# A 7x7 circular convolution on one core: scratch loads one group per round in the last tile, a weight group's preparation half a round earlier

## The chip, the core and the metric

The kernel runs on one core of a Trainium2 chip. The core has five engines with their own instruction streams: TensorE (PE), VectorE (DVE), ScalarE (ACT), GpSimd (POOL) and SyncE (SP), which here issues nearly all DMAs. Engines meet at semaphores. The time is the device time of one execution in microseconds (us), and lower is better. Before the change the median of eight runs is 281.08 us (280.29 to 283.76).

## The reference

```
H = W = 224;  C = 96;  K = 7          # x: (1, H, W, C) bf16, w: (K, K, C, C) bf16
wp = pad(w, H and W up to 224)
Yf = einsum('bhwi,hwio->bhwo', rfft2(x), rfft2(wp))
y  = irfft2(Yf)                       # bf16
```

So y is the circular convolution of a 224x224 image of 96 channels with a 7x7 kernel, 96 channels in and out, summed over the input channels.

## The kernel before

**The algorithm.** Rows (h) are cut in eight blocks of 28, each seen through a window of 34 rows. Along h the kernel uses a real Fourier transform of length 34, done as matmuls; it gives 17 frequencies s (`NS`), each with a real and an imaginary part, the first with two real ones. Along w it convolves directly, with the columns split in even and odd ones, which saves a quarter of the taps. A complex product is done with three real ones, so the transformed weights of a frequency take three slots: two parts, and their difference.

**The stages.** The width is cut in seven tiles t of 32 columns (`NT` = 7, `TL` = 6 is the last).

- *Weights*: `prep_jobs(gi)` (line 333) transforms the weights of a group of frequencies, 12 jobs of eight matmuls for groups 2 to 5, each copied from a PSUM bank to `WF`. `w_sub(gi, half)` (line 369) makes the difference slots on DVE, one half of the output channels each. `PGRP` lists six groups; group 5, the fifth after the first one, has frequencies 14 to 16.
- *A*, `a_jobs(t)`: transform of x along h, matmuls with the constant `Fm`, into `xf`.
- *J planes*, `jit(t, g)`: sums and differences of xf for three frequencies, three DVE instructions a group.
- *B*, `b_round(t, s, ...)` (line 485): all products of one frequency, 33 matmuls of 96 columns in two PSUM banks. ACT scales three of the sums (tile `tt_`), DVE makes `u` and `v`, and POOL (sometimes DVE) adds them to `yf`. After each third round `put_y` stores yf to scratch in DRAM (`scr`, in the last tile `scra` for rounds 0 to 8 and three `scrb` for the rest).
- *C*, `c_jobs(t)`: `load_t` reads the scratch back, turned round so that frequencies lie on partitions (tile `tt`), in six groups of two to four DMAs. `c_bank` does the inverse transform, a matmul with `Gm` (G in the code), copies the result to `yo`, and `put_o` stores it to the output.
- *The end*: C of the last tile is done differently. Rounds 0 to 8 are loaded from scra into `tl_a` (the xf buffer that is then free; line 828), rounds 9 to 16 from scrb by `load_b` into `tl_b`. Each of 16 output pieces is the sum of two matmuls, `first` with `GA` (built in Fm once A is over) and `second` with `GB`. Between the first eight `first` and the first `second` stand `WARM` filler matmuls (line 857), which add zeros.

**The order of work.** All engines run in program order, and the program is written round by round. Tiles 0 and 1 run interleaved, tile 1 four rounds (`LAG`) behind; a round r of the loop is then b_round of tile 0 and b_round of tile 1. The later tiles run alone. `add(a, b, jobs)` spreads a list of jobs over the half rounds a to b, and `pace` runs what is due, in the middle (`mid`) or at the end (`end`) of a b_round. `planes` are DVE jobs put between v and the POOL sum; the sum waits for them.

**The queue of scratch loads.** `queue_c(t)` puts the six groups of tile t into `pend`, at round 3 of the next tile, and `pump` (line 676) issues those for which one of the six tt buffers (`NTT`) is free. It runs again after every finished group of C. `late[0]` is 0 throughout. All DMAs, those on ACT's queue too, keep the program's order (`dorder`), and SP executes them one after another: one that waits holds those behind it. In the last tile rounds 9 to 14 are stored from ACT's queue (`puts`), the rest from SP's.

**What the change touches.** `WARM` (line 42), `pump` and `queue_c` (676 to 683), the call of pump in c_jobs (663), the half rounds of group 5's preparation and the round of its second difference (743, 744), and in the tile loop the Fm clear and its four DMAs (`g_parts`, line 617, called at 823), queue_c (821) and the loads of tl_a (828 to 833).

Of the kernel before, what the change touches and what calls it, by code (L numbers as in the profile page):

```python
# [16 lines left out]
NS = L // 2  # L17
# [21 lines left out]
CQ = {2: (10, 2), 3: (8, 4), 4: (6, 7), 5: (3, 9), 6: (1, 5)}  # L39
NXN = 2  # L40
NP2 = 0
WARM = 16


def slot(s, part):
    return part if s == 0 else 2 + 3 * (s - 1) + part
# [3 lines left out]
def kernel(  # L50
# [10 lines left out]
    TL = NT - 1  # L61
# [37 lines left out]
    def bank():  # L99
        return pools["psb"].tile([128, 512], F32, name="pb")  # L100
# [6 lines left out]
    def apart(key, zone, r, keep=None):  # L107
        for z, q in parts.setdefault(key, []):
            if z != zone and not (keep and z in keep) and q.engine != r.ins.engine:
                tc.declare_no_dep(r.ins, q, reason="disjoint parts of one tile")  # L110
        parts[key].append((zone, r.ins))
        return r

    def evac(out_ap, in_ap, n):
        if tail[0]:
            return tail_evac(out_ap, in_ap, n)
        cv, ca = 180 + 1.0 * n, 160 + 0.85 * n
        if clamp[0]:
            top = max(load.values()) - 2000
            for k in load:  # L120
                load[k] = max(load[k], top)
        if load["v"] + cv <= load["a"] + ca:
            load["v"] += cv
            return VE.tensor_copy(out=out_ap, in_=in_ap)
        load["a"] += ca
        return SE.copy(out=out_ap, in_=in_ap)
# [27 lines left out]
    SA = SL[1]  # L154
# [178 lines left out]
    def prep_jobs(gi):  # L333
        s0, s1 = PGRP[gi]
        ns = s1 - s0
        full = gi == 0
        if full:
            ncol = NSLOT_OF(s0, s1) * NTAP
        else:
            ncol = 2 * ns * NTAP  # L340
        nb = C // NB
        hb = NB // 2
        assert NB * ncol <= 512 and C2 % hb == 0

        def mk_(ob):
            def f():
                pw = bank()
                pv_ = pw[:, 0:NB * ncol].rearrange("p (k h q) -> p k h q", h=2, q=ncol)
                if full:
                    ev = Em[:, :, slot(s0, 0):slot(s0, 0) + ncol // NTAP, :].rearrange("p h a t -> p h (a t)")  # L350
                else:
                    ev = Em[:, :, slot(s0, 0):slot(s1 - 1, 2) + 1, :].rearrange("p h (s r) t -> p h s (r t)", r=3)[:, :, :, 0:2 * NTAP]
                for k in range(hb):
                    o = ob * hb + k
                    TE.matmul(pv_[:, k], lhsT=wqx[0:PW2, o:o + 127 * C + 1:C], rhs=ev, start=True, stop=True)
                pv_ = pv_[0:C]
                o0, o1 = ob * hb, (ob + 1) * hb
                if full:
                    wv = WF[0:C, slot(s0, 0):slot(s0, 0) + ncol // NTAP].rearrange("i a t (h o) -> i (a t) h o", h=2)
                    r = evac(wv[..., o0:o1], pv_.rearrange("i k h q -> i q h k"), NB * ncol)  # L360
                    apart(("W", gi), ob, r)
                    return r
                wv = WF[0:C, slot(s0, 0):slot(s1 - 1, 2) + 1].rearrange("i (s r) t (h o) -> i s (r t) h o", r=3, h=2)
                apart(("W", gi), ob, evac(wv[:, :, 0:2 * NTAP, :, o0:o1],
                      pv_.rearrange("i k h (s q) -> i s q h k", s=ns), NB * ncol))
            return f
        return [mk_(ob) for ob in range(nb)]
# [16 lines left out]
    def NSLOT_OF(s0, s1):  # L384
        return slot(s1 - 1, 2) + 1 - slot(s0, 0)
# [253 lines left out]
    def c_jobs(t):  # L639
        jobs = []  # L640
        for h in range(2):
            for gi in range(3):
                j0, nj = CG[gi]
                hold = {}

                def mk_(ks, done, h=h, gi=gi, j0=j0, nj=nj, hold=hold):
                    def f():
                        if ks[0] == 0:
                            hold["yo"] = yo_pool.tile([4 * B, PXC * C], BF16, name="yo")
                        tt = tt_tiles[(t, gi, h)]  # L650
                        yo = hold["yo"]
                        for k in ks:
                            c_bank(tt, yo, k, 3 if gi < 2 or h == 0 or k == 0 else 2)
                        if not done:
                            return
                        if gi < 2:
                            put_o(t, yo, 0, j0, nj, 8 * h, 8 * h + 8, 0)
                        else:
                            put_o(t, yo, 0, j0, nj, 6 * h, 6 * h + 6, 0)
                            for j, wa, wb, q0 in REST[h]:  # L660
                                put_o(t, yo, nj * B, j, 1, wa, wb, q0)
                        held[0] -= 1
                        pump()
                    return f
                if gi < 2:
                    jobs.extend((mk_((0, 1), False), mk_((2, 3), True)))
                else:
                    jobs.append(mk_((0, 1, 2), True))
        return jobs

    NTT = 6
    held = [0]
    late = [0]
    pend = []

    def pump():
        while len(pend) > late[0] and held[0] < NTT:
            load_t(*pend.pop(0))
            held[0] += 1

    def queue_c(t):
        pend.extend((t, i % 3, i // 3) for i in range(6))
        pump()

    def warm(n):
        p = bank()
# [13 lines left out]
    p1 = prep_jobs(1)  # L700
# [28 lines left out]
    def fills(qs, k):  # L729
        def f():  # L730
            for q in qs:
                pace(q, k)
        return f
# [4 lines left out]
    def add(a, b, jobs):  # L738
        qs.append([a, b, jobs, len(jobs)])

    for gi in range(1, len(PGRP)):
        b0 = PGRP[gi][0]
        add(max(0, 2 * b0 - (10 if gi < 5 else 8)), 2 * b0 - (4 if gi < 5 else 2) if gi > 1 else 1, prep_jobs(gi) if gi > 1 else p1)
        for h, (r, t) in enumerate(((max(b0 - 4, 2), 1), (b0 - 2, 0)) if 1 < gi < 5 else ((b0 - 3, 1), (b0 - 1, 0)) if gi == 5 else ((0, 0), (0, 0))):
            wsubs.setdefault((r, t if r >= LAG else 0), []).append(w_sub(gi, h))
    for t in range(2):
        scr_tiles[t] = dr_pool.tile([TW, NJ, NS, 4 * C], BF16, name="scr")
# [11 lines left out]
    for r in range(NS + LAG):  # L759
# [4 lines left out]
        for t in range(2):  # L764
            s = r - LAG * t
# [25 lines left out]
    gp = g_parts()  # L791
    for t in range(2, NT):
        if t == TL:
            scr_tiles[t] = None
            scr_tiles[(t, 0)] = dr_pool.tile([TW, NJ, SA, 4 * C], BF16, name="scra")
            for i in range(len(KB)):
                scr_tiles[(t, 1 + i)] = dr_pool.tile([TW, NJ, KB[i] // (2 * NJ), 4 * C], BF16, name=f"scrb{i}")
        else:
            scr_tiles[t] = dr_pool.tile([TW, NJ, NS, 4 * C], BF16, name="scr")
        qs = []  # L800
        if t + 1 < NT:
            add(0, 26, a_jobs(t + 1))
        nold, nnew = CQ[t]
        k1 = 2 * NS if t < TL else 2 * NS - 9
        k0 = 12 if t == 2 else 3
        km = max(13, k0 + -(-(k1 - k0) * nold // (nold + nnew)))
        add(k0, km, cj[:nold])
        cn = c_jobs(t - 1)
        cj = cn[nnew:]
        add(km, k1, cn[:nnew])  # L810
        plan = {}
        for g, (s0, s1) in enumerate(JGB):
            if g + 1 < len(JGB) or t + 1 < NT:
                plan[s0 if g + 1 < len(JGB) else s0 - 1] = g
        for s in range(NS):
            now = ()
            if s in plan:
                g = plan[s]
                now = jit(t, g + 1) if g + 1 < len(JGB) else jit(t + 1, 0)
            if s == 3:  # L820
                queue_c(t - 1)
            if t in (3, 4) and s < 12 or t == TL and s < 4:
                next(gp, None)
            if t == TL and s == SL[2] + 2:
                load_b(0, DE, 1)
            if t == TL and s == 0:
                late[0] = 0
            if t == TL and s == SA + 1:
                sv = scr_tiles[(TL, 0)].rearrange("w j s (r e) -> (j s r) w e", r=2)
                for g in range(2):  # L830
                    dma(tl_a[g], sv[g * KA:(g + 1) * KA])
                late[0] = 0
                pump()
            b_round(t, s, fills(qs, 2 * s), fills(qs, 2 * s + 1), bool(now) if t < TL else s >= NS - 2 or (s < 12 and bool(now)), now)
    tail[0] = 2
    load_b(1, DE, 1)
# [19 lines left out]
    live = {k: first(*k) for k in order[:8]}  # L856
    for _ in range(WARM):
        TE.matmul(live[order[7]].rearrange("p (a b) -> p a b", a=12), lhsT=Fm.rearrange("p r s j -> p (r s j)")[:, 0:M4],
# [48 lines left out]
```

## Time and profile before

The profiled execution took 281.09 us; its span, from the first to the last instruction, is 279.3.

| what | before |
|---|---|
| median of 8 runs | 281.08 us |
| profiled execution, its span | 281.09 us, 279.3 us |
| mean granted clock of PE | 0.972 |
| PE matmuls busy | 259.8 us (93%) |
| DVE busy | 237.8 us (85%) |
| ACT busy | 185.2 us (66%) |
| POOL busy | 97.7 us (35%) |
| SP's DMA queue, share of 16 engines | 56.5%, 43.78 MB |

A row of a timeline has start, length, engine, operation, tiles (out<-in), form and count; in brackets stands the engine's idle time before it and what ended it. "SPq" and "ACTq" are DMA issues, which the engine's busy time doesn't count. "x7" means seven instructions merged into one row. A row of the windows view has the stretch and its length, busy time and count of PE, PEld (weight loads), DVE, ACT and POOL, the granted clock of PE (1.00 is full), the busy share of the DMA engines, and GB/s. Names of ACT's tile carry a number, so tt__1896 is that of one b_round; tt without a number is the scratch tile of C. Two things read above the time itself: an engine's busy share is a mean over stages that have different limits, and the last 40 us belong to the last tile and its end.

### The profile page before, as it was taken

The numbers are of one execution on the slowest core, as the hardware profiler recorded it, in microseconds if no ns is written. First come the engines' busy times: TensorE is split into PE (matmuls) and PEld (weight loads), VectorE is DVE, ScalarE is ACT, GpSimd is POOL, SyncE is SP. The second block draws the span as 40 slices with busy tenths as digits, with TensorE's granted clock in tenths as the row PEclk, the third lists the DMA queues.
The fourth block names the chain that finished last, engine by engine and source line by source line (L and its number), as shares of the span: only waits on it lengthen the run. The fifth ranks groups of instructions, "written<-read, shape, count | busy, mean of one in ns | idle before, by whom it ended". The sixth has DMA issues, their size and how long they took to land.

```text
span 279.3 us, 11544 instructions
## 1 busy us (share of the span) xinstructions
PE 259.8 (93%) x4810; PEld 237.0 (85%) x4810; DVE 237.8 (85%) x500; ACT 185.2 (66%) x459; POOL 97.7 (35%) x134
## 2 busy tenths in 40 slices
PE   8399999999979999999999999999999999799692
PEld 3198899999979899998998998999989998798361
DVE  6279999999998899999878899778988899989423
ACT  5079986565615977977788677987688864462222
POOL 2741022366457335324322342332253224345000
PEclk9979999999999999999999999999999999999668
DMA  8696242111211569979686767795767642967856
GB/s 165 111 227 186 65 136 85 45 45 52 80 46 64 157 196 194 272 222 286 184 198 168 219 173 249 178 276 164 269 150 192 196 160 78 183 195 151 206 168 196
DMA packets 45284, 46.01 MB, mean 165 GB/s; under 512 B 33746, under 2 KB 35974, under 8 KB 45136
## 3 DMA queue, kind: packets, MB, share of 16 engines
q1 hardware_dynamic: 44816, 43.78, 56.5%
q10 hardware_dynamic: 416, 1.49, 2.4%
q8 instruction: 38, 0.62, 1.0%
q14 instruction: 14, 0.11, 0.2%
HBM read 23.92 MB, written 21.33 MB: 162 GB/s over the span
## 4 chain that ended last, share of the span: by engine, by line
PE 62%; DVE 18%; DMA 9%; ACT 7%; issue 3%; SPq 0%; DVEq 0%; ACTq 0%
PE pb L82 62%; DVE J L82 7%; DMA wq<-in_w_dram 4%; DVE v L82 4%; ACT xf L82 3%; DVE WF L82 3%; DVE u L82 3%; DMA out_dram<-yo 3%; ACT WF L82 2%; DMA tt<-scr 1%; DVE yf L82 1%; DVE xf L82 1%; SPq L82 0%; DVE tt L82 0%; DMA xn<-in_x_dram 0%
## 5 line engine op out<-in xcount | busy, mean ns | idle before, releaser
L82 PE MATMUL pb<-WF,J 96*128 96x96 bf16 x2898 | 165.5, 206 | 1.9 <-DVE J L82 0.8
L82 PEld LDWEIGHTS <-J 96*128 96x128 bf16 (+1 forms) x2910 | 142.5, 98 | 11.9 <-issue 4.5
L82 POOL TENSOR_TENSOR yf<-v,u 128x384 bf16<-128x384 f32 x87 | 85.9, 1005 | 142.6 <-issue 99.7
L82 ACT CAST xf<-pb 96x408 bf16<-96x408 f32 (+1 forms) x142 | 62.0, 492 | 4.7 <-PE pb L82 2.7
L82 DVE TENSOR_TENSOR J<-xf 96x1824 bf16<-96x1824 bf16 (+1 forms) x84 | 62.0, 776 | 0.1
L82 PE MATMUL pb<-WF,xf 96*128 96x96 bf16 x952 | 60.3, 206 | 1.6 <-DVE WF L82 1.4
L82 ACT CAST yo<-pb 84x384 bf16<-84x384 f32 (+1 forms) x122 | 52.0, 483 | 11.1 <-PE pb L82 6.0
L82 PEld LDWEIGHTS <-xf 96*128 96x128 bf16 x952 | 47.1, 98 | 2.0 <-issue 1.7
L82 PE MATMUL pb<-Fm,xn 118*128 118x136 bf16 x448 | 46.2, 222 | 0.3
L82 PE MATMUL pb<-tt,Gm 102*84 102x384 bf16 (+1 forms) x132 | 32.8, 331 | 5.1 <-DMA out_dram<-yo 3.0
L82 ACT CAST WF<-pb 96x480 bf16<-96x480 f32 (+1 forms) x58 | 30.3, 589 | 9.9 <-PE pb L82 9.8
L82 PEld LDWEIGHTS <-xn 118*128 118x128 bf16 x448 | 29.9, 98 | 1.3 <-issue 0.7
L82 PE MATMUL pb<-wq 98*128 98x120 bf16 (+1 forms) x288 | 23.9, 234 | 4.7 <-DMA xn<-in_x_dram 4.7
L82 PEld LDWEIGHTS <-wq 98*128 98x128 bf16 x288 | 21.2, 151 | 5.1 <-issue 5.1
L82 DVE TENSOR_TENSOR J<-J 96x912 bf16<-96x912 bf16 (+1 forms) x42 | 25.0, 594 | 0.0
L82 PEld LDWEIGHTS <-Gm 102*84 102x84 bf16 (+1 forms) x132 | 11.8, 117 | 6.8 <-DMA xf<-scra 3.2
L82 DVE TENSOR_TENSOR yf<-v,u 128x384 bf16<-128x384 f32 x24 | 16.2, 675 | 0.8
L82 DVE CAST xf<-pb 96x408 bf16<-96x408 f32 (+1 forms) x30 | 14.8, 531 | 0.1
L82 DVE CAST WF<-pb 96x480 bf16<-96x480 f32 (+1 forms) x14 | 8.4, 612 | 6.0 <-PE pb L82 5.6
L82 DVE CAST tt<-pb 112x384 bf16<-112x384 f32 x8 | 4.1, 554 | 7.0 <-PE pb L82 6.8
L82 DVE TENSOR_TENSOR WF<-WF 96x1440 bf16<-96x1440 bf16 x10 | 10.0, 1012 | 0.0
L82 PEld LDWEIGHTS <-wu 128*128 128x128 bf16 (+1 forms) x40 | 4.5, 114 | 6.0 <-issue 1.9
(393 smaller groups left out, 227.3 us busy)
## 6 DMA issues: line engine op xcount, KB each, us to landing
xn<-in_x_dram SPq DMA_DIRECT2D x13, 672.0 KB
scr<-yf SPq DMA_DIRECT2D x30, 288.0 KB
tt<-scr SPq DMA_DIRECT2D x24, 288.0 KB
out_dram<-yo SPq DMA_DIRECT2D x24, 252.0 KB
tt<-scr SPq DMA_DIRECT2D x12, 144.0 KB
out_dram<-yo SPq DMA_DIRECT2D x12, 126.0 KB
scr<-yf SPq DMA_DIRECT2D x6, 192.0 KB
scra<-yf SPq DMA_DIRECT2D x3, 288.0 KB
```

What stands on the lines that cost most here:

```text
L82: r = fn(*a, **k)
```

## The change

- **WARM** goes from 16 to 24.
- **Group 5's preparation** runs in the half rounds 19 to 24 instead of 20 to 25; its second difference runs with tile 1's b_round of round 12, no longer with tile 0's of round 13. Its first difference stays.
- **The last tile's scratch loads**: `late` goes; `pump(n)` issues at most n groups, and the calls in c_jobs pass `jlim[0]`, 6 in all tiles but 0 in the last. There, queue_c at round 3 issues one group, and each later round one more.
- **GA**: the clear of Fm and its four DMAs run in rounds 13 to 16 of the tile before, not in rounds 0 to 3 of the last.
- **tl_a's loads** are issued ahead of round 11 instead of round 10, and pump no longer follows them.

```diff
-WARM = 16
+WARM = 24
...
                         held[0] -= 1
-                        pump()
+                        pump(jlim[0])
...
     held = [0]
-    late = [0]
+    jlim = [NTT]
     pend = []
 
-    def pump():
-        while len(pend) > late[0] and held[0] < NTT:
+    def pump(n=NTT):
+        while pend and held[0] < NTT and n:
             load_t(*pend.pop(0))
             held[0] += 1
-
-    def queue_c(t):
+            n -= 1
+
+    def queue_c(t, n=NTT):
         pend.extend((t, i % 3, i // 3) for i in range(6))
-        pump()
+        pump(n)
...
-        add(max(0, 2 * b0 - (10 if gi < 5 else 8)), 2 * b0 - (4 if gi < 5 else 2) if gi > 1 else 1, prep_jobs(gi) if gi > 1 else p1)
-        for h, (r, t) in enumerate(((max(b0 - 4, 2), 1), (b0 - 2, 0)) if 1 < gi < 5 else ((b0 - 3, 1), (b0 - 1, 0)) if gi == 5 else ((0, 0), (0, 0))):
+        add(max(0, 2 * b0 - (10 if gi < 5 else 9)), 2 * b0 - (4 if gi < 5 else 3) if gi > 1 else 1, prep_jobs(gi) if gi > 1 else p1)
+        for h, (r, t) in enumerate(((max(b0 - 4, 2), 1), (b0 - 2, 0)) if 1 < gi < 5 else ((b0 - 3, 1), (b0 - 2, 1)) if gi == 5 else ((0, 0), (0, 0))):
...
         if t == TL:
+            jlim[0] = 0
...
             if s == 3:
-                queue_c(t - 1)
-            if t in (3, 4) and s < 12 or t == TL and s < 4:
+                queue_c(t - 1, 1 if t == TL else NTT)
+            elif t == TL and s > 3:
+                pump(1)
+            if t in (3, 4) and s < 12 or t == TL - 1 and s >= NS - 4:
                 next(gp, None)
             if t == TL and s == SL[2] + 2:
                 load_b(0, DE, 1)
-            if t == TL and s == 0:
-                late[0] = 0
-            if t == TL and s == SA + 1:
+            if t == TL and s == SA + 2:
                 sv = scr_tiles[(TL, 0)].rearrange("w j s (r e) -> (j s r) w e", r=2)
                 for g in range(2):
                     dma(tl_a[g], sv[g * KA:(g + 1) * KA])
-                late[0] = 0
-                pump()
```

## The prediction, made before the changed kernel was seen

> **What bounds the kernel now.** I read the chain of waits first. From 93.95 us TensorE (PE) runs on, with short breaks, until the last tile. Its end, in the chain's answer for the stretch from 235 us (start, length, what):
>
> ```profile
> 240.66 12.78 PE pb L82 x266
> 253.44 7.31 DMA out_dram<-yo
> 260.75 2.76 PE pb L82 x7
> 263.51 0.02 issue
> 263.53 10.10 PE pb L82 x40
> ```
>
> PE is the bound until about 257.8, then something of the DMA queues is, then 40 matmuls, of which 16 are the WARM filler. The timeline of that stretch says what was waited for:
>
> ```profile
> 256.49 1.30 PE L82 MATMUL pb<-tt,Gm 102*84 102x384 bf16 x7
> ...
> 258.29 1.94 DVE L82 CAST yo<-pb 84x384 bf16<-84x384 f32 x4
> 259.77 0.33 ACTq L82 DMA_DIRECT2D scrb<-yf  x1
> ...
> 260.22 1.61 ACT L82 CAST yo<-pb 84x384 bf16<-84x384 f32 x4 [3.66 <-DMA xf<-scra]
> 260.75 1.63 PE L82 MATMUL pb<-tt,Gm 102*84 102x384 bf16 x4 [2.95 <-DMA out_dram<-yo]
> ```
>
> ScalarE (ACT) had nothing to compute after 256.56, yet its casts began at 260.22: ahead of them stands its scrb store, whose sums were there at 256.37. The operands in the trace give the reason. Every DMA raises one of eight semaphores, taken in turn in program order, and is not issued before the previous owner, the eighth DMA before it, has landed. For this store that is the first xf<-scra load, which landed at 259.70. VectorE (DVE) is held the same way: its casts stop after four, until the store of a yo buffer lands at 262.93. The last scrb store on SP (262.29; sums ready 258.37) waits for the second xf<-scra load (262.23). Everything at the end hangs on when the scra loads run and who is eighth behind them.
>
> The windows of the clock's own length (3.41 us) show the second half:
>
> ```profile
> 256.65:260.06 3.41, 1.15 (x8) 0.71 (x6) 3.27 (x9) 0.00 (x0) 0.00 (x0) 1.00 1.00 179
> 260.06:263.47 3.41, 2.73 (x7) 1.01 (x7) 0.64 (x2) 2.08 (x5) 0.00 (x0) 0.50 0.94 261
> ...
> 266.89:270.30 3.41, 3.41 (x12) 2.23 (x12) 0.00 (x0) 0.00 (x0) 0.00 (x0) 0.50 0.74 248
> ```
>
> The first number after the length is PE's busy time, the third from the end the granted clock. After a window with 1.15 us of work the clock fell to half, and stayed there 10.24 us. So the 16 fillers went at 0.32 us each (265.08 to 270.20), though the last load they cover landed at 268.66. The end is bound by fillers at half clock, behind a start that ACT's wait had made late.
>
> **The change, part by part.**
>
> *Scratch loads one group per round.* SP's queue in the last tile:
>
> ```profile
> 236.02 0.36 SPq L82 DMA_DIRECT2D scra<-yf  x1
> 236.49 9.83 SPq L82 DMA_DIRECT2D tt<-scr  x15
> ...
> 247.27 1.12 SPq L82 DMA_DIRECT2D scra<-yf  x1
> ...
> 248.94 0.35 SPq L82 DMA_DIRECT2D scra<-yf  x1
> 252.27 1.08 SPq L82 DMA_DIRECT2D xf<-scra  x2
> ```
>
> No instruction is added. The first eight loads (groups 1 to 3) keep their place, for nothing stands between them in the queue, and SP is held by the 236.02 store in either kernel. PE's 1.25 us wait for the first group (ended at 240.52) therefore stays: gain nothing. Then the round-5 scra store comes ahead of groups 4 to 6: its POOL sums end at 241.09, so it goes at about 241.1 instead of 247.27. Behind it: seven loads (246.32 - 241.36 = 4.96 us) and the first output store (0.35). With 0.36 to 1.12 for the scra store and 0.3 of gaps the round-8 scra store (sums at 246.19) goes at 247.1 to 247.9 instead of 248.94. It took 3.28 us to land, so the scra loads can go at 250.4 to 251.2; I take 250.8, against 252.27. Groups 4 to 6 are read from 256.49 on; if each came 2 us later than before (landed by 249.6), it would cost nothing.
>
> *The scra loads one round later in the program.* This moves them behind the second output store (casts end at 248.07), which SP then has time for before 250.8. So the order behind them becomes: three output stores, scrb store, scrb load, scrb store (ACT), scrb store (SP). The eighth before ACT's blocked store is now that output store, issued near 248.2; at the 3.01 us of the one before it, it lands near 251.2. ACT's wait of 3.2 us goes. The SP store's eighth is the first scra load: 250.8 + 7.43 (its time before) = 258.2, no wait. DVE's buffer wait goes with the early output store.
>
> What is late next: SP itself. Before, the DMA behind the two scra loads was stuck in its issue for 4.84 us, to 258.28. The same is to be expected 1.5 us earlier, to 256.8; two more output stores (1.2) and the scrb load (0.37) bring SP to 258.5, and the last scrb store goes at 258.6 instead of 262.29. It lands in 3.28 us, or about 4.6 if it queues behind the scrb load's packets now just ahead: 261.9 to 263.2, taken as 262.6. The last load follows and took 3.08: data at **265.9**, against 268.66.
>
> PE: with ACT free at 256.6 its casts run ahead; DVE's six casts from 258.29 at 0.485 us end at 261.2. The last bank for the eight first matmuls comes then; they end near 261.4, against 265.28.
>
> *WARM 24.* At full clock a matmul of 384 columns came every 0.16 us (from 270.42 on), so 24 take 3.84: 261.4 to 265.3, hidden by the data at 265.9. The cover is 0.6 us; without it each extra matmul costs 0.16, or 0.32 at half clock. Second matmuls start at 265.9 against 270.20: **4.3 us**.
>
> Is the clock kept? Columns against what full clock passes: windows after which it fell had 28%, 14% and 1%; the emptiest after which it stayed had 56%. With ten of the eleven inverse matmuls and some firsts in the window to 260.06 I get 50 to 66%, and no later than 261.5 the fillers start. Nearer to 56 than to 28: kept.
>
> *Preparation and second difference half a round earlier.* Same 12 jobs of eight matmuls, same difference. The place is this:
>
> ```profile
> 78.34 0.54 DVE L82 SCALAR_TENSOR_TENSOR v<-tt__1896,pb 128x384 f32<-128x384 f32 x1
> 78.80 1.47 DVE L82 TENSOR_TENSOR WF<-WF 96x1440 bf16<-96x1440 bf16 x1
> ```
>
> PE waits 1.44 us for that end (80.28). The difference moves ahead of u and v of 1896, to 78.07, where u starts now. Alone it takes 0.89 (median), beside POOL's sum 1.47; that sum now covers only to 78.5, so it ends near 79.4 and PE starts 0.9 earlier. But DVE has no pause to 84.3 (5.00 of every 5 us from 30 to 80), and the J planes that PE needs next (82.2) and after (86.9) come only 0.05 and 0.3 earlier. I keep 0.3, bounds 0 and 0.9. The preparation's 0.5 us on PE and two casts (1.0) on ACT move from about 74.3 to 62.5, beside DVE's backlog of 2 us and more; nothing. If the backlog is smaller, 0.2 lost.
>
> *The Fm clear and its four DMAs* go to the end of the tile before: 0.20 on POOL and four issues of 0.8 on SP, which has nothing to issue in 224.70 to 226.74 and 228.8 to 231.39. Nothing; if a store is held, at most the 0.8 of one issue.
>
> **Sum**, against the profiled execution (281.09, of it 279.3 span and 1.8 around it, equal to the median of 281.08): 281.09 - 4.3 - 0.3 = **276.5**.
>
> **Rivals.**
>
> *Clock still falls* (17%). The transfers come early, but a window with too few columns is found; these windows run free of the kernel, so it may differ by execution. Fillers from 261.7 at 0.32 end at 269.4. Here the Trainium skill ("TensorE: Matmul & The Clock Gate", Part 1, "What's actually happening") has a rule: half clock after a whole idle window, full again after one busy window of 3.4 us. By the row, half clock lasted three windows, two of them full: all 24 at 0.32, 280.0. By the rule the clock is back by 266.89, 16 at 0.32 and 8 at 0.16 end at 268.2: 278.8. I take the middle, 279.4. For it: the 28% window wasn't idle and still fell. Against: the first matmuls fill just that window.
>
> *WARM costs, PE's start isn't earlier* (11%, slower). Should the scra loads be no earlier, or ACT and DVE still be held, the firsts end at 265.28 as before and eight fillers are added: 8 x 0.16 if the clock is back at 270.30, 8 x 0.32 if not, +1.3 to +2.6, less 0.3: 282.8. The point from which it decides: 270.20 - 24 x 0.32 = 262.5; firsts that end later lose. Against: the semaphore turn follows from program order.
>
> *The data stays late* (8%). PE starts early, but SP's stuck issue lasts longer, the last scrb store goes at 262 again and data lands near 268.7: 281.09 - 1.5 - 0.3 = 279.3. PE would then idle 3.4 us ahead of its last 24 matmuls and may do them at half clock, 24 x 0.16 = 3.8 more at most; with 1.1 of it, 280.4. For it: the trace shows no cause of that 4.84 us issue. Against: SP does the same number of issues, and starts them earlier.
>
> **How the numbers follow.** My case 64%: 276.5, own range 275.2 to 278. The range adds the clock rival and most of the late data, 275.2 to 280.5; the slower rival is left out. A change under 0.5% (1.4 us) can't be told from none: faster is below 279.7, slower above 282.5. Faster: my case and over half of the clock rival, 0.75; slower: two thirds of the third, with strays, 0.09; the rest 0.16.
>
> **What would show it.** Right: ACT's casts on yo from about 257, no PE pause of 3 us there, the last scrb store on SP before 260, clock 1.0 until the second matmuls, fillers at 0.16; near 79 us a PE wait under 0.7. Wrong: PE still idle near 258 to 260, fillers at 0.32, second matmuls after 268, or the scra loads issued at 252 again.

## The result, and the profile after

| | before | after |
|---|---|---|
| median (lowest to highest, executions) | 282.03 us (279.43 to 288.82, 32) | 279.39 us (276.12 to 281.83, 11) |
| profiled execution, its span | 281.09 us, 279.3 us | 277.84 us, 276.0 us |
| its mean granted clock | 0.972 | 0.983 |

The ratio of after to before is **0.9891 [0.9853, 0.9929]**: faster by 1.1%, 3.06 us of 281.08. A repetition (e8, below) gave 0.9952 [0.9920, 0.9983], 1.35 us. The ratio leaves out the executions that took over 1.5% longer than the fastest of their kernel; the medians count all. So the change helps, by 1.3 to 3 us where 4.6 were forecast. The median lies in the forecast's range of 275.2 to 280.5, but above the 275.2 to 278 of its own case: it is inside by the width that the rivals had added.

The chain of waits of the changed kernel (start, length, what), from the last tile on:

```profile
241.26 17.15 PE pb L82 x348
258.41 0.56 DVE yf L82
258.97 0.02 issue
258.99 4.43 DMA scrb<-yf
263.42 0.02 issue
263.43 2.85 DMA xf<-scrb
266.29 0.14 issue
266.42 3.88 PE pb L82 x22
```

The output store of 7.31 us that stood in the chain before is gone, and so are the 16 fillers. PE runs through to the last sum of yf (258.97), and from there only two transfers lie between it and the last 22 matmuls. That sum is the last one of the convolution.

The timeline of the same stretch:

```profile
256.75 0.41 ACT L82 ACTIVATE tt__7230<-pb 128x288 f32<-128x288 f32 x1 [0.99 <-DVE v L82]
256.99 0.33 ACTq L82 DMA_DIRECT2D scrb<-yf  x1
...
257.62 2.22 ACT L82 CAST yo<-pb 84x384 bf16<-84x384 f32 x5 [0.46 <-DMA out_dram<-yo]
...
258.88 2.87 DVE L82 CAST yo<-pb 84x384 bf16<-84x384 f32 x6
258.99 0.35 SPq L82 DMA_DIRECT2D scrb<-yf  x1
...
259.48 2.64 PE L82 MATMUL pb<-xf,Fm 72*112 72x384 bf16 x8
...
261.96 4.06 PE L82 MATMUL pb<-xn,Fm 118*112 118x384 bf16 x24
...
266.42 0.83 PE L82 MATMUL pb<-xf,GB 128*112 128x384 bf16 x4 [0.40 <-DMA xf<-scrb]
```

ACT's casts on yo follow its last scaling after 0.46 us, where they had waited 3.66; the scrb store ahead of them goes at once. The eight first matmuls stand at 259.48, the 24 fillers behind them end at 266.0, and PE then waits 0.40 us for the data. The windows of the clock (PE, PEld, DVE, ACT and POOL, then granted clock, DMA share, GB/s) show that it holds:

```profile
256.12:259.54 3.42, 3.25 (x39) 2.24 (x37) 3.25 (x9) 2.19 (x6) 0.84 (x1) 1.00 1.03 250
259.54:262.95 3.41, 2.99 (x15) 1.68 (x16) 2.21 (x5) 0.30 (x1) 0.00 (x0) 1.00 0.90 249
262.95:266.36 3.41, 3.07 (x19) 2.20 (x17) 0.00 (x0) 0.00 (x0) 0.00 (x0) 1.00 0.74 222
266.36:269.78 3.42, 3.36 (x20) 2.65 (x21) 2.60 (x5) 2.47 (x6) 0.00 (x0) 1.00 0.55 157
```

Before, the stretch 260.06 to 270.30 ran at 0.50. SP's queue in the last tile, from its timeline:

```profile
241.72 0.76 SPq L82 DMA_DIRECT2D scra<-yf  x1
242.58 3.09 SPq L82 DMA_DIRECT2D tt<-scr  x4
245.76 0.35 SPq L82 DMA_DIRECT2D out_dram<-yo  x1
246.21 1.51 SPq L82 DMA_DIRECT2D tt<-scr  x3
248.38 0.35 SPq L82 DMA_DIRECT2D scra<-yf  x1
248.82 0.35 SPq L82 DMA_DIRECT2D out_dram<-yo  x1
252.22 1.03 SPq L82 DMA_DIRECT2D xf<-scra  x2
```

The round-5 scra store now goes ahead of seven scratch loads, and the second output store ahead of the two scra loads, as the program's order has it.

**Where the 3.25 us between the two profiled executions come from.** PE's milestones between 37.9 and 241 us, those beside group 5's preparation (60 to 95 us) apart, stand 0.55 to 0.60 us later in after, for a reason at the very start: the clock was at half from 13.78 to 20.61 us in after, from 14.3 to 17.71 in before. Nothing of the change is there. Second matmuls: 270.20 before, 266.42 after, which is 3.78, or 4.38 measured from the milestones. From there to the end of the span: 9.13 before (279.33 - 270.20), 9.58 after (276.0 - 266.42); output stores of the last C groups landed as late as 269.02, and one of the end's store issues took 1.28 us. So 4.38 - 0.60 - 0.45 = 3.33, the difference of the spans.

### The profile page after: what moved, and what is told of

Read it like the earlier page. It is cut to its first block, busy times and chain, and to the rows that moved or that the text cites. A ratio compares the mean times of both kernels' runs of the same rounds, so it can differ in the third digit from the quotient of the medians.

```text
span 276.0 us, 11563 instructions
## 1 busy us (share of the span) xinstructions
PE 260.0 (94%) x4818; PEld 237.4 (86%) x4818; DVE 238.2 (86%) x500; ACT 185.6 (67%) x459; POOL 97.8 (35%) x134
## 4 chain that ended last, share of the span: by engine, by line
PE 59%; DVE 22%; DMA 8%; ACT 6%; issue 2%; SPq 0%; DVEq 0%; ACTq 0%
PE pb L82 59%; DVE J L82 9%; DVE v L82 5%; DMA wq<-in_w_dram 4%; ACT xf L82 3%; DVE u L82 3%; DVE WF L82 2%; ACT WF L82 2%; DMA scrb<-yf 2%; DMA tt<-scr 1%; DVE yf L82 1%; DMA xf<-scrb 1%; DVE xf L82 1%; SPq L82 0%; DVE tt L82 0%
## 5 line engine op out<-in xcount | busy, mean ns | idle before, releaser
L82 PE MATMUL pb<-tt,Gm 102*84 102x384 bf16 (+1 forms) x132 | 32.1, 326 | 2.3 <-DMA tt<-scr 1.3
L82 PE MATMUL pb<-wq 98*128 98x120 bf16 (+1 forms) x288 | 24.6, 239 | 3.0 <-DMA xn<-in_x_dram 2.7
L82 PE MATMUL pb<-wu 128*128 128x512 bf16 x32 | 10.0, 487 | 1.1 <-DVE ct L82 1.1
```

Of the source, the lines that this page charges most:

```text
L82: r = fn(*a, **k)
```

## The experiments

Ratios are to the kernel before, run on the same chip as the kernel. "Columns" means the share of a 3.41 us window's matmul columns that full clock would pass, counted from the records by the matmuls' starts. A diff is against before or after, as said.

**e1: the order alone** (against before). tl_a's loads go one round later in the program, and nothing else.

```diff
-            if t == TL and s == SA + 1:
+            if t == TL and s == SA + 2:
```

> The kernel before, with one line changed: tl_a is loaded ahead of round 11 instead of round 10, which puts the second output store ahead of these loads in the order of the DMAs. Scratch loads, preparation and 16 fillers are as before. Theory A (the semaphore turn): this alone frees ACT and DVE at the end; ACT's casts on yo follow its last scaling within 1.5 us, PE's pause of 2.95 us near 258 goes, the first matmuls end 3 us earlier, and the kernel is faster by 2 to 4 us (the data then comes some 0.5 us later than in the changed kernel, and with 16 fillers PE waits for it 2 to 3 us). Theory B (the spread of the scratch loads relieves SP, and that is what frees the end): no change beyond 0.5 us, PE still pauses for about 3 us.

Measured: 1.0015 [0.9976, 1.0054], no gain, where Theory A had 2 to 4 us. Its timeline shows that the order freed ACT, as Theory A said, and what PE then waited for:

```profile
258.61 0.33 ACTq L82 DMA_DIRECT2D scrb<-yf  x1
...
259.24 2.23 ACT L82 CAST yo<-pb 84x384 bf16<-84x384 f32 x5 [0.46 <-DMA xf<-scra]
...
269.02 1.50 PE L82 MATMUL pb<-xf,GB 128*112 128x384 bf16 x4 [2.15 <-DMA xf<-scrb]
```

ACT's casts start 1 us sooner than before and without the 3.66 us pause. But the 16 fillers end at 266.9, the data comes only at 268.9, and PE waits 2.15 us. The windows tell the price:

```profile
77.75:81.16 3.41, 1.97 (x46) 1.86 (x44) 3.41 (x8) 0.41 (x1) 2.38 (x3) 1.00 0.14 52
81.16:84.58 3.42, 3.42 (x48) 3.42 (x45) 2.55 (x6) 0.82 (x2) 2.03 (x3) 0.50 0.11 41
265.48:268.90 3.42, 1.39 (x9) 0.83 (x7) 0.00 (x0) 0.00 (x0) 0.00 (x0) 1.00 0.74 222
268.90:272.31 3.41, 3.29 (x11) 2.29 (x12) 1.67 (x3) 1.59 (x4) 0.00 (x0) 0.50 0.55 161
```

The window with the wait has 33% of the columns, and the last 22 matmuls then run at half clock: 5.4 us from first to last instead of 3.9. So the order frees the engines, and PE waits for the data, which lands at 268.88, beside 268.66 before. How much of the lost gain that is can't be said from this trace, for its convolution ended 2.2 us later than before's (258.88 against 256.65). The first two rows are one reason, a second fall near 80 us, behind the wait for group 5's difference (49% of the columns); it cost 1.3 us and belongs to what the preparation's move touches.

**e2: 24 fillers alone** (against before).

```diff
-WARM = 16
+WARM = 24
```

> The kernel before with 24 fillers instead of 16 and nothing else. Theory A: PE's start at the end is as late as before and the clock falls there, so the eight fillers are added to the time: slower by 1.3 us (clock back before the last eight) to 2.6 us (not back). Theory C (the fillers are what brings the gain, by bringing the clock back before the last 24 matmuls): faster by 1 us or more.

Measured: 1.0047 [1.0014, 1.0080], 1.3 us slower. That is the price of eight fillers on the path at full clock, 8 x 0.16 = 1.28, and the size of the slower rival. Its trace doesn't show the path: it is of one of the shorter executions (280.37, the median is 282.90) in which ACT's store was held less long and the clock didn't fall ahead of the second matmuls, so that the fillers end at 268.04 and PE waits for the data:

```profile
263.97 4.07 PE L82 MATMUL pb<-xn,Fm 118*112 118x384 bf16 x24
269.10 0.83 PE L82 MATMUL pb<-xf,GB 128*112 128x384 bf16 x4 [1.06 <-DMA xf<-scrb]
```

So the loss is measured, and its cause is argued.

**e3: one more DMA behind tl_a's loads** (against after). It writes a small tile that nobody reads, and shifts the turn of the eight semaphores by one.

```diff
+    spare = cpool.tile([16, 32], BF16, name="spare")
...
                     dma(tl_a[g], sv[g * KA:(g + 1) * KA])
+                dma(spare, x[0, 0:16, 0, 0:32])
```

> The changed kernel with one more DMA, of 1 KB into a tile that nobody reads, issued right behind the two loads of tl_a. It makes the first of these loads, instead of the second output store, the eighth DMA before ACT's blocked scrb store. Theory A: ACT's casts on yo wait again until the first load has landed (near 258 to 260 in place of 257.6), PE pauses again, and the time rises by 0.3 to 3 us depending on when the load lands; in the trace ACT's idle time before its casts is ended by DMA xf<-scra. Theory B: a DMA of 1 KB costs its issue on SP, below 0.5 us, and ACT's casts stay where they are.

Measured: 0.9968 [0.9935, 1.0000], a smaller gain than either ratio of after, though its interval overlaps that of the repetition. Its timeline:

```profile
257.44 0.41 ACT L82 ACTIVATE tt__7232<-pb 128x288 f32<-128x288 f32 x1 [0.99 <-DVE v L82]
...
258.68 0.33 ACTq L82 DMA_DIRECT2D scrb<-yf  x1
...
259.12 2.01 ACT L82 CAST yo<-pb 84x384 bf16<-84x384 f32 x5 [1.27 <-PE pb L82]
...
261.13 0.35 SPq L82 DMA_DIRECT2D scrb<-yf  x1
```

ACT is free at 257.85, yet its store goes at 258.68, which is 0.08 after the first tl_a load landed (258.60). The last scrb store goes at 261.13, 0.06 after the second one landed (261.07); its sums were done at 259.67. The engine named in the bracket of the casts (PE) is not what held them. Second matmuls start at 268.35 instead of 266.42; less the 0.69 us by which this execution was already later at ACT's last scaling (257.44 against 256.75), that is 1.2 us. That a DMA waits for the eighth before it is shown by this run: one DMA more, and each store waits for another owner. That the transfer of one KB costs 1.2 us is not shown: from the end of the convolution to the second matmuls takes 10.4 us here and 9.2 in after, but up to 11.0 in other traces with after's own end (table below).

**e4: 16 fillers in after.**

```diff
-WARM = 24
+WARM = 16
```

> The changed kernel with 16 fillers instead of 24. The data for the second matmuls comes near 266.3 in the trace of the changed kernel, the firsts end near 262, and 16 fillers at full clock end near 264.6. Theory A: PE waits about 1.7 us instead of 0.4 for the same data; if the clock stays, the time is the same within 0.5 us; if it falls in some executions, the last 24 matmuls go at up to twice 0.16 us and the median is 0.5 to 2 us slower. Theory C: the fillers bring most of the gain, so the time goes back to that of the kernel before, 3 us slower than the changed kernel.

Measured: 0.9933 [0.9903, 0.9964], not to be told from after. The trace shows what the eight were for:

```profile
263.54:266.96 3.42, 1.16 (x8) 0.65 (x5) 0.00 (x0) 0.00 (x0) 0.00 (x0) 1.00 0.87 235
266.96:270.37 3.41, 3.23 (x11) 2.23 (x12) 1.67 (x3) 1.53 (x4) 0.00 (x0) 0.50 0.54 163
```

PE waits 2.44 us for the data, the window has 28% of the columns, and the last matmuls take 5.37 us instead of 3.87. In one trace that is 1.5 us; in the ratio it is at most a part of it.

**e5: the preparation's edits alone** (against before), **and e6: after without them.** The two edits of the change at group 5, put in or taken out:

```diff
-        add(max(0, 2 * b0 - (10 if gi < 5 else 8)), 2 * b0 - (4 if gi < 5 else 2) if gi > 1 else 1, ...
+        add(max(0, 2 * b0 - (10 if gi < 5 else 9)), 2 * b0 - (4 if gi < 5 else 3) if gi > 1 else 1, ...
-        ... ((b0 - 3, 1), (b0 - 1, 0)) if gi == 5 ...
+        ... ((b0 - 3, 1), (b0 - 2, 1)) if gi == 5 ...
```

> The kernel before with group 5's preparation and second difference half a round earlier, nothing else. In the traces of the two runs that kept the old place, the 1.44 us wait near 80 us left a 3.41 us window with 49% of full columns, and the clock fell to half for the next 3.41 us, which put PE 1.3 us back; in the profile of the kernel before, whose windows lay otherwise (62%), it did not fall. Theory D (the step's worth is the clock): the wait is cut in several of 0.3 to 0.5 us, no window there is under 55%, the clock does not fall near 80 us, and the median is 0.3 to 1.3 us lower, though PE reaches 142 us no earlier than in an execution in which the clock stayed. Theory E (as forecast: the step is worth 0.3 us and the clock has no part in it): the same within 0.5 us.

> The changed kernel with group 5's preparation and second difference in their old place. Theory D: the 1.44 us wait near 80 us is back; in executions whose windows lie so, the clock falls there, and the median is 0.3 to 1.3 us above that of the changed kernel run beside it. Theory E: the same within 0.5 us. The end of the kernel, from the last inverse matmuls on, is as in the changed kernel.

Measured: e5 1.0048 [1.0021, 1.0075], slower by 1.3 us; e6 0.9984 [0.9948, 1.0020], beside 0.9952 [0.9920, 0.9983] for after on the same chip. So the edits cost in one kernel and perhaps help in the other, where the intervals overlap. Neither theory foresaw a loss in e5, and its cause is open: its profiled execution lost clock in the last tile, where none of the two edits is:

```profile
239.13:242.54 3.41, 1.60 (x32) 1.37 (x30) 3.38 (x8) 0.67 (x2) 1.95 (x2) 1.00 1.09 222
242.54:245.95 3.41, 3.41 (x41) 3.12 (x39) 2.44 (x5) 1.78 (x5) 0.41 (x1) 0.50 0.56 128
```

Here the wait for the first scratch group (1.81 us) and one for a J plane (0.60) fell in one window: 40% of the columns.

**e7: the spread of the scratch loads and GA's move alone** (against after: 16 fillers, tl_a's loads ahead of round 10, the preparation as before).

```diff
-WARM = 24
+WARM = 16
...
-            if t == TL and s == SA + 2:
+            if t == TL and s == SA + 1:
```

> The kernel before with the scratch loads one group per round, and the clear of Fm with its four DMAs in the tile before; tl_a's loads ahead of round 10, 16 fillers and the preparation as before. Theory A (the semaphore turn frees the end): ACT's scrb store still waits for the first tl_a load, which goes 0.5 to 1 us earlier than before, so ACT's casts, PE's restart and the second matmuls come at most 1 us earlier and the median is the same within 1 us. Theory B (the relief of SP frees the end): faster by 2 us or more, with ACT's casts near 257.

Measured: 1.0003 [0.9970, 1.0036], no gain, though tl_a's loads go at 251.11 in it, 1.2 us sooner than before. In its profiled execution the clock fell at 239.82 and at 263.72. The first fall made PE 3.1 us late, so that the two loads had landed (256.00 and 258.43) before the sums of the stores behind them were done, and both stores went with their sums (258.80 and 260.80). So the wait that Theory A expected here isn't in this trace, and what the old order makes of the earlier loads when PE is on time isn't shown.

**e8: after again.**

> The changed kernel again, beside the three others, as their measure and for one more trace of its clock. All theories: 2 to 4 us faster than the kernel before; second matmuls within 1 us of the last load's landing, clock 1.0 from the start stage to the second matmuls in most executions.

Measured: 0.9952 [0.9920, 0.9983], less than the 2 to 4 us expected. Its profiled execution took 284.53 us, the longest of 22 with a median of 279.65. It is no measure of the kernel, but shows what can make an execution long:

```profile
210.53:213.94 3.41, 0.60 (x8) 0.49 (x9) 2.60 (x5) 0.34 (x2) 0.00 (x0) 1.00 0.94 189
213.94:217.35 3.41, 3.41 (x40) 3.20 (x37) 0.91 (x2) 1.75 (x5) 0.00 (x0) 0.50 0.83 208
```

PE waited 3.21 us at 213 us for a scratch load of the tile before, then had half clock for a window; that put it 4.9 us back. The clock fell again at 268.55, and the 24 fillers ran at half clock. A wait of C for its scratch is a place in which this kernel can lose time twice over. That led to the next runs.

**f1: C's jobs later** (against after). The jobs of C that read the previous tile's scratch begin no earlier than half round 16 of a tile.

```diff
-        add(km, k1, cn[:nnew])
+        add(max(km, 16), k1, cn[:nnew])
```

> The changed kernel, in which the new inverse-transform jobs of the last two tiles begin at half round 16 instead of 13, so that the first group of scratch loads has 2.6 us more before PE reads it. In all traces so far PE waits 1.2 to 1.8 us for that group near 241 us, with 0.6 for a J plane 3 us earlier, and in three of ten the clock fell for 3.4 to 6.8 us behind it. Theory F (this wait, and the fall of the clock that it can bring, are what the changed kernel loses most between executions): the wait is below 0.3 us, no fall near 240, the median is 1 to 2.5 us below that of the changed kernel in the earlier calls (ratio to before 0.985 to 0.991). Theory G (the end waits for the DMAs in any case): the wait goes but the second matmuls start no earlier, ratio as the changed kernel's, 0.989 to 0.995.

Measured: 0.9880 [0.9833, 0.9927], median 277.19. From 200 us to the end of its trace PE waits once, 0.8 us for u; the waits for scratch are gone, no clock falls between 19 and 271 us, and second matmuls start at 264.62. Wait and fall go together here, so their shares of the gain aren't told apart.

**f2: f1 with 48 instead of 32 fillers at the start, and f4: these fillers in after.**

```diff
-    for _ in range(4):
+    for _ in range(6):
```

> As the run before, and 48 instead of 32 filler matmuls at the very start. In all traces the start fillers end near 9 to 12 us, the first weight matmuls come near 14, and the clock stands at half for 3.4 to 6.8 us from there, during which PE does some 4 us of work. Theory F, extended: the clock is full at the first weight matmul in most executions, these take half as long, and A's first matmuls come 1 to 2 us earlier: ratio 0.003 to 0.007 below the run before. Against it: ACT's copies bound that stretch, then below 0.5 us.

> The changed kernel with 48 instead of 32 start fillers and nothing else. Theory F, extended: 1 to 2 us below the changed kernel (ratio to before 0.984 to 0.991). If ACT's copies bound the start: within 0.5 us of the changed kernel.

Measured: f2 **0.9857 [0.9817, 0.9898]**, median 276.64 (276.30 to 277.66); f4 0.9863 [0.9818, 0.9908], median 277.28 (276.09 to 280.39). The rows of the granted clock in tenths, over 40 slices of the span, for after, then f2:

```profile
PEclk9959999999999999999999999999999999999997
```

```profile
PEclk9999999999999999999999999999999999999998
```

The 5 in the third slice is gone. With 32 start fillers PE runs out of work at 11.0 us in after and waits 2.74 us for x (4.65 from 9.6 in before), and in all twelve traces with 32 the clock is then at half for 3.4 to 6.8 us. With 48 it is busy until x is there, in both traces, and from the first weight transform to the first convolution it takes 10.85 us (f2) and 10.61 (f4). With 32 that was 12.31 in after, the longest, but 11.19 to 12.18 in the other traces (11.27 before), so by this stretch the fillers gain 0.3 to 1.7 us. f2 is 0.0023 below f1, inside their intervals. Its six executions lie within 1.4 us of each other.

**f3: C's jobs later, in before.** The same edit as f1.

> The kernel before with the same later inverse jobs and nothing else. Theory H (the end of the kernel before is set by the DMAs, so what PE gains or loses ahead of it is given back): PE ends the last round 1 us or more earlier relative to the first, ACT's wait for the first tl_a load grows by as much, and the median stays within 0.5%. Theory F alone: it gains as much as in the changed kernel, 1 us or more.

Measured: 0.9972 [0.9949, 0.9995]: 0.8 us. ACT's store waits in its trace until 258.33 for a tl_a load that landed at 258.26, and the clock fell at 80.81 and 261.72. That fits Theory H: what C's delay wins early, the end as it was before mostly takes back.

f1, f2 and f4 ran on one chip, with overlapping intervals; which is best isn't settled, and after ran on other chips, so that f2 is set beside it only by the ratios to before (0.9857 against 0.9891 and 0.9952). Not tried: the order and the 24 fillers together without the spread, GA's move alone, and fillers in the middle of the kernel.

## Why the prediction was right, and what it sized wrong

The mechanism at the end held step by step. After's times below are less the 0.6 us by which its start was later:

| step | predicted | measured |
|---|---|---|
| wait for the first scratch group | 1.25, stays | 1.26 |
| round-5 scra store goes | 241.1 | 241.1 |
| round-8 scra store goes | 247.1 to 247.9 | 247.8 |
| it lands after | 3.28 | 3.82 |
| tl_a's loads go | 250.8 | 251.6 |
| ACT's and DVE's waits at the end | gone | gone (0.46 left) |
| issue behind tl_a's loads | stuck 4.84 | 2.73 |
| last scrb store goes | 258.6 | 258.4 |
| last load has landed | 265.9 | 265.7 |
| second matmuls | 265.9 | 265.8 |
| clock until then | full | full |
| wait near 79 us | 1.44 to 0.5, gain 0.3 | 1.44 to 0.48, gain 0 |

Two errors of the data path met and cancelled: the round-8 store took 0.54 us longer to land, and SP's issue was stuck 2.1 us less. The last scrb store hung on neither in the end, but on the sums. That was luck of this execution: in e6, which has the same end, SP was stuck 4.98 us,

```profile
253.03 4.98 SPq L82 DMA_DIRECT2D out_dram<-yo  x1
...
259.38 0.51 SPq L82 DMA_DIRECT2D scrb<-yf  x1
```

the last scrb store had to wait for SP, and went 2.8 us behind the end of the convolution instead of 1.7. The 24 fillers have cover as said: they end 0.4 us ahead of the data.

**The preparation's 0.3 us came out as its lower bound.** The 1.44 us wait became small ones, in the waits of PE from 60 to 95 us (total, times, longest):

```profile
PE pb L82 <- DVE J L82: 0.9, 3, 0.3
PE pb L82 <- DVE WF L82: 0.5, 1, 0.5
PE pb L82 <- DVE u L82: 0.3, 1, 0.3
```

They make 1.69 us, as against 1.63 before. DVE has no pause there, as the prediction had noted, so a difference that comes earlier makes the J planes come later by the same: an engine that is the bound is not made shorter by order. What the move did change, the prediction hadn't asked: with the old place the clock fell near 80 us in three of six traces (e1, e2, f3; 1.3 to 1.4 us each), with the new one in none of eight. As e5 is slower, no gain is shown by that.

**What was mis-sized is the sum's own base.** 281.09 - 4.3 - 0.3 takes the gain at the end off one execution and leaves all else as it was there. Between the two profiled executions the end gave its 4.3 (measured 4.38), but 0.60 was lost at the start by a longer half clock, 0.45 behind the second matmuls, and 0.3 wasn't there: 276.5 + 1.35 = 277.85, the profile's 277.84. And after's other executions are not like its profile: their median is 1.55 us above it. The traces show two things that differ between executions.

The first is the clock. After's executions have mean clocks from 0.967 to 0.992 (281.74 and 276.12 us), and mostly the lower clock has the longer time. One fall of 3.41 us takes 0.5 x 3.41 / 276 = 0.006 of the mean clock; the predicted trace, with one such fall at the start, would have 0.99, and after's executions have a median of 0.980, e8's 0.983. So the forecast left in the base the falls that before's profile had, and counted on none but the first in after. The rival in which the clock still falls named the mechanism, but looked for it at the end alone; that its 279.4 is the measured median is chance, for at the end of after's profile the clock stayed. The runs that take such falls away (f1, f2, f4) reach the 276.6 to 277.3 that the forecast had for the change alone; f1 and f2 take away a wait as well.

The second is the end itself. The end of the convolution is the end of the last matmul on WF:

| trace | convolution ends | second matmuls | between |
|---|---|---|---|
| before | 256.65 | 270.20 | 13.6 |
| e2, e5, f3: scratch loads and tl_a's loads as before | 257.7 to 259.5 | 268.6 to 269.2 | 9.7 to 10.9 |
| after | 257.26 | 266.42 | 9.2 |
| e6, e8, f1, f2, f4: end as in after | 255.6 to 262.3 | 264.6 to 273.3 | 8.6 to 11.0 |

In e2, e5 and f3 PE came 1.1 to 2.9 us later than in before's profile, the first tl_a load landed no later (258.3 to 259.5, against 259.70), and the stretch was shorter. So 4.4 us is the gain over an execution in which PE came early and then waited for the transfers; where PE comes late, the old end makes up for part of it, and less is there to gain. How the shortfall divides between the clock and the end isn't shown.

**Why no part brings the gain alone.** Measured are the ratios: 1.0015, 1.0047, 1.0048 and 1.0003 for the parts, 0.9891 and 0.9952 for the whole. The reason is argued. In before's profile two paths reach the second matmuls at about the same time: PE's, through ACT's blocked store and the fillers at half clock (270.20), and the data's, through the last scrb store (268.66). An edit that frees the first alone leaves PE waiting for the second, as e1's 2.15 us show. For the spread alone no such trace exists: in e7's neither store waited for a load.

The slower rival was wrong in its premise, since PE's start did come earlier, and its price is of the size that e2 measured. The late-data rival had its stuck issue in e6 (4.98 us), and there the data landed at 266.89, later than the forecast's 265.9 but not as late as the rival's 268.7, and PE waited 0.74 us for it.

## What to carry to other kernels

Before you take one of two paths' delay away, work out when the other one arrives: the gain is only up to there, and edits that each gain nothing alone can gain together, as here. A wait for transfers also hides delays of the engine ahead of it, so a gain read off an execution in which that engine came early can be too large for the others. A wait of PE can cost almost twice its length, once by itself and once by the clock (near 80 us in e1, 1.4 and 1.3 us), so ask of each wait in how full a window it falls, and give such places work (fillers while the first data comes) or later consumers. A profiled execution shows one draw of these falls; a forecast of a median has to ask what the draw leaves out on both sides.

## What the runs showed of the hardware

- **The clock falls without idle windows.** Between 19 and 270 us of the 14 traces it fell behind windows with 16, 28 (three times), 33, 39, 40, 42, 49 (three times) and 52% (twice) of the columns, a matmul counted where it starts, and stayed behind 50% (once), 53, 55, 55, 55, 56% and more. No one share divides the two: outside that stretch it stayed behind 31% (twice, near 9 us) and 42% (twice, behind 270 us). The rule weighed in the prediction (a whole idle window) is too mild here: waits of 1.4 to 2.4 us in one window were enough.
- **It comes back late, and by no fixed time.** Half clock lasted 3.41, 6.83 or 10.24 us, though PE had work all through the later windows. So neither value of the clock rival could be chosen from one trace. Nor do the windows start with the kernel: the start fillers begin at 1.06 us in all traces, and the clock first rises at 3.98 to 7.02.
- **The same issue behind the same two loads** was stuck 2.45 (e7) to 4.98 us (e6) in the 14 traces: 4.84 before, 2.73 in after, 2.90 in e3. e6 has the end of after, so the change doesn't set it. What does is open.
- **A 1 KB transfer that nobody reads** changed what two stores waited for (e3: they went 0.08 and 0.06 us after the landing of the eighth DMA before them): what counts of a DMA added is also its place in the program.
